# Ten products of zeros instead of six in TensorE's first step

## The chip, the cores and the metric

The kernel runs on one core of one Trainium2 chip. The metric is device time in microseconds (us) of one execution; the median of several runs is compared. A core has five engines that work side by side, each with its own queue of instructions in a fixed order: TensorE (PE in the profile) multiplies, VectorE (DVE) and ScalarE (ACT) work elementwise, GpSimd (POOL) and SyncE (SP) here mostly issue transfers (DMA). Engines wait for one another through semaphores.

## The reference

The computation mixes two branches over 2048 rows of 512 numbers, weighted row by row by a gate. Branch A is a filter in the frequency domain (a 2D real FFT, a product with complex weights, the inverse FFT). Branch B is two dense layers with a GELU between them.

```python
x = A_x                                              # 1 x 2048 x 512
g = sigmoid((x * gate_w).sum(-1, keepdims=True))
X = rfft2(x) * (A_w_r + 1j * A_w_i)                  # 2048 x 257
a = irfft2(X, s=(2048, 512))
h = gelu(x @ B_w1 + B_b1)                            # 512 -> 1792
b = h @ B_w2 + B_b2                                  # 1792 -> 512
out = g * a + (1 - g) * b
```

## The kernel before

The rows are tiled in 16 blocks of 128 (`NJ = 16`); four classes c = 0 to 3 hold the blocks j with j % 4 == c. The hidden width 1792 is cut in 14 slices f of 128. To keep float32 accuracy in a format that TensorE multiplies at one pass, each operand is split into a high and a low part (names ending in h and l): x into mxh and mxl, slice f of the first weight matrix into wa{f}h and wa{f}l. ScalarE or VectorE rounds the high part out of the loaded numbers, VectorE subtracts to get the low part, and a product is the sum of three: high by high, low by high, high by low. `ph` is the PSUM block in which the first dense layer of one slice accumulates. After it ScalarE applies the bias and the GELU (L904) and splits the result into g_{f}h (L466), and VectorE makes g_{f}l (L467). The FFT branch is done with matrix products too: folding adds on VectorE (`eo` and `w`, L571 and L574) and products into `pd` and `py`.

All work is recorded as steps. A table of numbers, ORDER, sets the order in which the steps are written out, and SLOTS says which buffer each tile gets. So every engine's queue is fixed by hand, and nothing is sorted at run time.

What matters here is the start. VectorE writes a tile of zeros (`zero`, L484), and TensorE's first step, `warm`, multiplies it by itself six times into a block `none` that nobody reads: 512 columns each. Ten more steps (`FILL`) hold one smaller product of zeros each, 256 columns; ORDER puts eight of them right after `warm` and two between the first groups for slice 0 and those for slice 1. Meanwhile the first transfers come in: four 128-row blocks of x that make up class 0 (blocks 0, 4, 8 and 12), the first weight slices (`war`, split into wa0h and so on, L890 to L896) and the first slices of the second matrix (`wb`). The weight for slice 0 comes in two halves, each turned into its half of wa0h by VectorE (L891). The first real products, eight of 128 columns, need both halves and blocks 0 and 4 of x; then come groups of four products with 256 columns (half of class 0), first for slices 0 and 1 with blocks 0 and 4, then the same with blocks 8 and 12, and from slice 2 on products of 512 columns.

All of TensorE's products outside branch B's last part are written by one helper, `mm` (L416), so that line stands beside most of TensorE's rows, and the tile names tell them apart.

Of the kernel before, what the change touches and what calls it, by code (L numbers as in the profile page):

```python
# [345 lines left out]
def tile_kernel(ctx: ExitStack, tc: tile.TileContext, xt, xc, w1, w2, b1, b2, x0g, wf, wrev, out, consts):  # L346
# [68 lines left out]
    def mm(ps, w, x, start, stop):  # L415
        pe.matmul(ps, w, x, start=start, stop=stop)  # L416
# [6 lines left out]
    def bcast(ap, *ns):  # L423
        return bass.AP(tensor=ap.tensor, offset=ap.offset, ap=[list(ap.ap[0]), *[[0, n] for n in ns], list(ap.ap[1])])
# [62 lines left out]
      -1).table = "gelu"  # L487

    def warm():
        for _ in range(6):  # L490
            mm(none.ap(), zero.ap(), bcast(zero.ap(), 4), True, True)

    add("pe", 2.65, 0.1, warm, [zero], [none], -2)

    for _ in range(FILL):
# [783 lines left out]
```

## Time and profile before

| | us |
|---|---|
| median of 3 runs | 366.76 |
| the three runs | 364.87, 366.76, 367.12 |
| span of the profiled execution, first to last instruction | 364.1 |
| TensorE's first product of zeros starts | 1.05 |
| its first real product starts | 7.04 |
| ScalarE's first GELU starts | 15.58 |

The profiled execution's own device time is not given with the profile; its span is what the profile tells of it. The profile gives the busy time of each engine, 40 slices of the span, the chain of work that ended last, and groups of instructions. A timeline lists the instructions of an engine by time: start and duration in us, engine, line, operation, output and inputs, the shapes, how many were merged into the row, and in brackets how long the engine sat idle before and what it waited for. A row that merges several products shows the shape of the first one. A product's duration includes its way through the array, so products that follow each other overlap in time, and the distance between starts tells the rate.

### The profile page before, as it was taken

The page shows a single profiled execution, that of the slowest core. Times are in us where ns is not written, and L with a number is a line of the kernel's source. Part 1 is how long each engine was busy: PE and PEld are TensorE (multiplying, and loading weights), DVE is VectorE, ACT ScalarE, POOL GpSimd, SP SyncE. Part 2 cuts the span into 40 slices and gives each one's busy share as a digit, 9 for nine tenths or more (in the row PEclk, how much of TensorE's full clock was granted, in tenths as well). Part 3 has the DMA queues.
Part 4 walks back from the last instruction along what each step waited for, and adds up shares of the span by engine and source line. Part 5 has one row for each costly group of instructions (what it writes and reads, how often), then busy time and mean ns, then how long its engine had stood idle before and what let it go on. Part 6 is the DMA issues. An engine that isn't in the chain of part 4 may idle for free.

```text
span 364.1 us, 5722 instructions
## 1 busy us (share of the span) xinstructions
PE 358.0 (98%) x1808; PEld 305.1 (84%) x1808; DVE 330.0 (91%) x745; ACT 254.1 (70%) x471; POOL 70.3 (19%) x91
## 2 busy tenths in 40 slices
PE   7999999999999999999999999999999999999996
PEld 6988898899878888888888888888888888889885
DVE  3588998998997899999999899999988889999995
ACT  4596579798988722257567865899999988676200
POOL 1011000121012132111023430010323221103220
PEclk9999999999999999999999999999999999999999
DMA  7997868568859699999978987164868858479878
GB/s 251 352 309 171 275 206 230 160 179 192 222 126 220 155 242 195 249 325 241 251 176 138 190 146 213 44 164 125 160 103 157 117 88 193 110 207 200 219 181 245
DMA packets 46494, 70.34 MB, mean 193 GB/s; under 512 B 5376, under 2 KB 19200, under 8 KB 46464
## 3 DMA queue, kind: packets, MB, share of 16 engines
q1 hardware_dynamic: 34592, 48.93, 42.2%
q0 software_dynamic: 11440, 20.72, 36.6%
q10 hardware_dynamic: 432, 0.33, 0.3%
q8 instruction: 14, 0.23, 0.2%
q14 instruction: 16, 0.13, 0.1%
HBM read 48.32 MB, written 19.41 MB: 186 GB/s over the span
## 4 chain that ended last, share of the span: by engine, by line
PE 97%; DMA 1%; SPq 0%; DVE 0%; issue 0%; DVEq 0%
PE ph L416 22%; PE poB L416 21%; PE po L416 21%; PE ux L1090 10%; PE nu L1090 8%; PE pd L416 4%; PE pz L416 4%; PE py L416 3%; PE pa L416 3%; DMA war<-in_w 1%; SPq L505 0%; PE pown L416 0%; PE none L416 0%; SPq L890 0%; DVE wa0h L891 0%
## 5 line engine op out<-in xcount | busy, mean ns | idle before, releaser
L904 ACT ACTIVATE ph<-ph,b1t 128x512 f32<-128x512 f32 x28 | 18.3, 654 | 17.1 <-PE ph L416 17.1
L407 POOL DMA_DIRECT2D bacc<-oB x16 | 14.2, 909 | 53.5 <-ACT oB L982 53.0
L803 ACT ACTIVATE sw<-y,al 64x512 f32<-64x512 f32 x32 | 22.9, 720 | 1.2 <-DVE y L669 0.7
L407 POOL DMA_DIRECT2D bacc<-o x16 | 14.9, 991 | 41.0 <-ACT o L982 38.2
L765 DVE TENSOR_TENSOR m<-y,wf 128x514 f32<-128x514 f32 x32 | 21.5, 691 | 0.2
L982 ACT ACTIVATE o<-po 128x512 f32<-128x512 f32 x16 | 9.3, 597 | 17.3 <-PE po L416 17.3
L632 ACT ACTIVATE y<-pys 64x257 f32<-64x257 f32 x32 | 13.4, 418 | 6.4 <-DVE pys L629 5.7
L416 PEld LDWEIGHTS pz<-tg,pq 128*128 128x128 f32 x128 | 16.8, 191 | 1.2
L416 PE MATMUL pd<-cf,w 128*128 128x129 f32 x128 | 17.8, 274 | 0.0
L416 PEld LDWEIGHTS pd<-cf,w 128*128 128x128 f32 x128 | 16.8, 190 | 0.8
L1090 PE MATMUL nu<-xf,wa0h 128*128 128x512 f32 x56 | 17.5, 394 | 0.0
L416 PE MATMUL py<-zb,tf 128*128 128x258 f32 x96 | 17.2, 294 | 0.0
L416 PE MATMUL pz<-tg,pq 128*128 128x128 f32 x128 | 17.2, 274 | 0.0
L810 DVE SCALAR_TENSOR_TENSOR pq<-y,al,sw 128x256 f32<-128x256 f32 x32 | 14.8, 478 | 0.9 <-ACT sw L803 0.7
L416 PEld LDWEIGHTS py<-zb,tf 128*128 128x128 f32 x96 | 14.3, 190 | 1.2
L416 PEld LDWEIGHTS pa<-zb,ci 128*128 128x128 f32 x96 | 13.9, 188 | 1.4
L416 PE MATMUL pa<-zb,ci 128*128 128x256 f32 x96 | 14.8, 283 | 0.0
L607 DVE TENSOR_TENSOR zb<-pd,zb 128x256 fp32r<-128x256 f32 x32 | 12.8, 419 | 0.8 <-ACT zb L604 0.7
L574 DVE TENSOR_TENSOR w<-eo 128x256 f32<-128x256 f32 x32 | 12.8, 419 | 0.3
L571 DVE TENSOR_TENSOR eo<-xf 128x256 f32<-128x256 f32 x32 | 12.9, 419 | 0.0
L823 DVE TENSOR_TENSOR zb<-pz,zb 128x512 fp32r<-128x512 f32 x16 | 10.9, 687 | 2.1 <-ACT zb L822 2.1
L604 ACT ACTIVATE zb<-pd 128x256 fp32r<-128x256 f32 x32 | 12.0, 382 | 1.1 <-PE pd L416 0.5
(700 smaller groups left out, 1277.6 us busy)
## 6 DMA issues: line engine op xcount, KB each, us to landing
wf<-in_wf SPq DMA_DIRECT2D x16, 257.0 KB
bacc<-o POOLq DMA_DIRECT2D x16, 256.0 KB, 6.1
bacc<-oB POOLq DMA_DIRECT2D x16, 256.0 KB, 5.4
xf<-in_xt SPq DMA_DIRECT2D x14, 256.0 KB
wr<-in_w SPq DMA_DIRECT2D x14, 256.0 KB, 4.4
tf<-tf SPq DMA_DIRECT2D x16, 192.0 KB, 4.5
bacc<-o SPq DMA_DIRECT2D x8, 256.0 KB, 5.5
ba<-bacc SPq DMA_DIRECT2D x8, 256.0 KB, 7.8
```

The costliest lines, as they stand in the source:

```text
L407: return add("pool", 2.3 * kb / 340, 3.4, lambda: nc.gpsimd.dma_start(dst(), src(), accum_op=ALU.add), reads, writes, rank)
L416: pe.matmul(ps, w, x, start=start, stop=stop)
L571: v(lambda s=s, op=op: vec.tensor_tensor(eo.ap()[:, s], x.ap()[:, 0:2], x.ap()[:, 2:4], op=op), 256, [x], [(eo, s)], feed)
L574: v(lambda s=s, op=op: vec.tensor_tensor(w.ap()[:, s], eo.ap()[:, :, 0], eo.ap()[:, :, 1], op=op), 256, [eo], [(w, s)], feed)
L604: a(lambda c=c: act.activation(segs(xh, c), both(c), AF.Copy), 256, [ps[c]], [(xh, c)], 0)
L607: v(lambda c=c: vec.tensor_tensor(segs(xl, c), both(c), segs(xh, c), op=ALU.subtract), 256, [ps[c], (xh, c)], [(xl, c)], 0)
L632: a(lambda o=o, i=i: act.activation(Y[j].ap()[o:o + HP, 1], pys.ap()[i:i + HP, 1], AF.Copy), 257, [(pys, 1)], [(Y[j], 1 + k)], 0, more=0.1)
L765: v(lambda mk=mk, k=k, y=y, w=w: vec.tensor_tensor(mk.ap(), y.ap(), w.ap()[:, k:k + 1, :ND].to_broadcast([P, 2, ND]), op=ALU.mult), 514, [ ...
L803: a(lambda sw=sw, y=y, o=o, i=i: act.activation(sw.ap()[o:o + HP], y.ap()[i:i + HP, ::-1, :HD], AF.Copy, scale=al.ap()[i:i + HP, 0:1]), 51 ...
L810: v(lambda sw=sw, pq_=pq_, y=y, j=j, k=k, op=op: vec.scalar_tensor_tensor(pq_.ap()[:, k], y.ap()[:, k, :HD], al.ap()[:, 1 + j:2 + j], sw.a ...
L904: a(lambda: act.activation(ps.ap(), ps.ap(), AF.Gelu_apprx_tanh, bias=b1t.ap()[:, f:f + 1]), 600, [b1t], [ps]).table = "gelu"
L1090: pe.matmul(o.ap(), w(wi, e), FX[j].ap()[:, xi, e], start=first, stop=k == 5, skip_group_check=not start)
```

## The change

One number is changed: `warm` issues ten products of 512 columns instead of six. All ten read `zero` and write `none`, as the six do. The step keeps its place, its two buffers and its planned cost.

```diff
     def warm():
-        for _ in range(6):
+        for _ in range(10):
             mm(none.ap(), zero.ap(), bcast(zero.ap(), 4), True, True)
 
     add("pe", 2.65, 0.1, warm, [zero], [none], -2)
```

TensorE's queue at the start of the program, before (a row is a run of equal products; x6 counts them, and the numbers at the end of a name are those of the buffers):

```order
L1271 UNCONDITIONAL_BRANCH
L416 MATMUL none<-zero 128x512 x6
L416 MATMUL none<-zero 128x256 x8
L416 MATMUL ph_0_137<-mxh_95,wa0h 128x128 x8
L416 MATMUL ph_0_137<-mxl_115,wa0h 128x256 x4
```

And now:

```order
L1271 UNCONDITIONAL_BRANCH
L416 MATMUL none<-zero 128x512 x10
L416 MATMUL none<-zero 128x256 x8
L416 MATMUL ph_0_141<-mxh_99,wa0h 128x128 x8
L416 MATMUL ph_0_141<-mxl_119,wa0h 128x256 x4
```

Only the count in the second row differs; the buffers' running numbers shift by four. Every later row of TensorE's queue, and every row of the other four queues, is the same but for such numbers.

## The prediction

> **What bounds the kernel now.** I read the page first: the busy table, the 40 slices, and the chain that ended last.
>
> ```profile
> PE 358.0 (98%) x1808; PEld 305.1 (84%) x1808; DVE 330.0 (91%) x745; ACT 254.1 (70%) x471; POOL 70.3 (19%) x91
> PE   7999999999999999999999999999999999999996
> PEclk9999999999999999999999999999999999999999
> PE 97%; DMA 1%; SPq 0%; DVE 0%; issue 0%; DVEq 0%
> ```
>
> TensorE is busy in every slice but the first and the last, and 97% of the chain is its work. The PEclk row reads full speed from the start; the durations below contradict it for the first 13 us, and I go by the durations. Next I read TensorE's timeline from the start of the span (columns: start, duration, instruction, count, idle time before it and what ended that).
>
> ```profile
> 1.05 4.64 PE L416 MATMUL none<-zero 128*128 128x512 f32 x14 [1.05 <-DVE zero L484]
> 7.04 1.94 PE L416 MATMUL ph<-mxh,wa0h 128*128 128x128 f32 x8 [1.35 <-DVE wa0h L891]
> 8.78 1.16 PE L416 MATMUL ph<-mxl,wa0h 128*128 128x256 f32 x4
> 9.73 1.05 PE L416 MATMUL ph<-mxh,wa0l 128*128 128x256 f32 x4
> 10.59 0.63 PE L416 MATMUL none<-zero 128*128 128x256 f32 x2
> 11.02 1.05 PE L416 MATMUL ph<-mxh,wa1h 128*128 128x256 f32 x4
> 11.87 1.05 PE L416 MATMUL ph<-mxl,wa1h 128*128 128x256 f32 x4
> 12.72 0.91 PE L416 MATMUL ph<-mxh,wa1l 128*128 128x256 f32 x4
> 13.47 0.64 PE L416 MATMUL ph<-mxh,wa0h 128*128 128x256 f32 x4
> 13.94 0.64 PE L416 MATMUL ph<-mxh,wa1h 128*128 128x256 f32 x4
> ...
> 16.34 0.40 PE L416 MATMUL ph<-mxh,wa2h 128*128 128x512 f32 x1
> 16.57 0.40 PE L416 MATMUL ph<-mxl,wa2h 128*128 128x512 f32 x1
> ```
>
> The starts tell the rate, since products overlap. Four products of 256 columns take 11.87 - 11.02 = 0.85 us, which is 0.213 us each; after 13.47 four take 0.47 us, 0.118 us each. The group that starts at 12.72 takes 0.75 us: three at the slow rate and one at the fast. So TensorE runs at about half rate until about 13.35 us, and no row before that is fast. The first stretch of unbroken work (1.05 to 5.69, 4.64 us) was not enough to end it; the second, from 7.04 on, was, after 13.35 - 7.04 = 6.31 us. Between them lie the 1.35 us in which TensorE waits for the second half of wa0h. That gap costs twice: its own length, which no edit here can win back because the weight is late, and, if unbroken work is what lifts the rate, a new start of that count.
>
> **The change part by part.** It adds four products of 512 columns to TensorE's queue between the sixth and the eight small ones, and nothing else; no wait, no DMA and no tile is added.
>
> *Their length.* At the slow rate 512 columns cost 2 x 0.213 = 0.425 us by spacing, so four cost 1.70 us. The other end is the whole duration of one such product, as if none overlapped:
>
> ```profile
> L416 PE MATMUL none<-zero x2: 628/628/628, 2.9 to 3.4; 128*128 128x512 f32 x2
> ```
>
> That gives 4 x 0.628 = 2.51 us, but two of them start 0.4 to 0.5 us apart in this same row, so I take 1.70. The stretch of zeros then ends at 5.69 + 1.70 = 7.39. Its last 0.20 us is drain (the two products at 10.59 last 0.63 us, and the next group starts 0.43 us after them), so the first real product can start at 7.19, against 7.04 before. Between 5.69 and 7.04 the four stand where nothing ran; 0.15 us of them lies on the path.
>
> *The rate.* TensorE now works without a gap from 1.05 us. The trace bounds how long that must last: 4.64 us was too short, 6.31 us was enough. So the full rate should come between 5.69 and 1.05 + 6.31 = 7.36 us, not at 13.35. If it comes early in that range, the small zero products shorten too, and the first real product starts at 7.04 as before. I take the late end, 7.36.
>
> [...]
>
> *What full rate is worth.* Now the inputs of the first real products decide, so their rows on VectorE and ScalarE:
>
> ```profile
> 6.60 0.29 DVE L891 CAST wa0h<-war 128x256 fp32r<-128x256 f32 x1 [2.17 <-DMA war<-in_w]
> 6.81 1.29 DVE L560 TENSOR_TENSOR mxl<-xf,mxh 128x512 fp32r<-128x512 f32 x2
> 8.35 0.69 DVE L896 TENSOR_TENSOR wa0l<-war,wa0h 128x512 fp32r<-128x512 f32 x1
> 9.28 0.69 DVE L896 TENSOR_TENSOR wa1l<-war,wa1h 128x512 fp32r<-128x512 f32 x1
> 9.88 1.29 DVE L560 TENSOR_TENSOR mxl<-xf,mxh 128x512 fp32r<-128x512 f32 x2
> ```
>
> None of these waits for TensorE, so they stay where they are. From the end of one to the product that needs it I allow 0.15 us (6.89 to 7.04 in the rows). Step by step: the eight products of 128 columns, 1.74 us before, take 0.87 and end at 8.06. The next four need mxl, ready at 8.10, and so start at 8.25 and end at 8.73. The next four need wa0l, ready at 9.04: they start at 9.19 and end at 9.66. The two zeros take 0.24, to 9.90. Three groups for wa1 take 0.47 each, to 11.31 (wa1l is ready at 9.97). That is the point that stands at 13.47 before: **2.16 us earlier**. The six groups after it are at full rate in both; the second pair of mxl is ready at 11.17 and is wanted about 12.3. So ph for wa2 starts at 14.18 instead of 16.34. Two waits for data (0.19 and 0.46 us) are inside this number, and they make it insensitive: a release anywhere up to about 7.5 us ends at the same 9.19.
>
> *Does it last to the end?* What is late next is whatever TensorE then reaches sooner. The rows where the other engines hand over:
>
> ```profile
> 15.58 0.66 ACT L904 ACTIVATE ph<-ph,b1t 128x512 f32<-128x512 f32 x1 [3.87 <-PE ph L416]
> 17.34 0.63 ACT L894 ACTIVATE wa3h<-war 128x512 fp32r<-128x512 f32 x1
> 16.90 0.69 DVE L467 TENSOR_TENSOR g_1l<-ph,g_1h 128x512 fp32r<-128x512 f32 x1 [3.20 <-ACT g_1h L466]
> 18.00 0.69 DVE L896 TENSOR_TENSOR wa3l<-war,wa3h 128x512 fp32r<-128x512 f32 x1 [0.41 <-ACT wa3h L894]
> 19.54 0.39 PE L416 MATMUL ph<-mxh,wa3l 128*128 128x512 f32 x1
> 6.17 0.33 SPq L893 DMA_DIRECT2D war<-in_w  x1
> 10.60 0.43 SPq L478 DMA_DIRECT2D xf<-in_xt  x1
> 22.94 0.62 ACT L559 ACTIVATE mxh<-xf 128x512 fp32r<-128x512 f32 x1
> tf<-tf SPq DMA_DIRECT2D x9, 192.0 KB, 5.3
> 7.00:20.00 13.00, 12.96 (x71) 12.35 (x72) 9.29 (x20) 8.80 (x15) 1.11 (x2) 1.00 1.06 366
> 120.00:364.00 244.00, 240.44 (x1178) 202.77 (x1176) 228.83 (x483) 159.92 (x280) 53.86 (x62) 1.00 0.79 179
> ```
>
> ScalarE had waited 3.87 us for TensorE's first finished block, and VectorE 3.20 us for ScalarE behind it. Both idle times exceed 2.16 us, so both queues move forward with TensorE. Among what moves is wa3h and wa3l, which stand behind those waits and are ready 0.85 us before TensorE wants wa3l (18.69 against 19.54); this margin stays if all three move together. Transfers are the part that does not move: from 7 to 20 us the DMA engines are full (share 1.06 in the stage row). The weight for wa3 is issued at 6.17 and used at 17.34, an x block is issued at 10.60 and used by ScalarE at 22.94, so 11 to 12 us lie between; loads of this kind land in about 5.3 us. With 2.16 us taken away the cover holds. Later the DMA share falls to 0.79 and TensorE is busy 240.44 of 244 us, so there is room to keep the lead. The loss on the way is bounded by 0 and 2.16 us; as both idle times and both transfer margins are larger than the shift, I take 0.
>
> **Sum.** The profiled execution spans 364.1 us, 2.66 less than the median of 366.76; its own device time is not given, and I take 2.66 as what lies around the span. 364.1 - 2.16 + 2.66 = **364.6 us**, 0.6% below the median. A difference of 1% is about what a measurement of this kernel can tell from none, so this counts as no change.
>
> **The rivals.**
>
> *A. The forecast:* release before 7.5 us, lead kept. 364.6 us, with its own range 364.0 to 365.4.
>
> *B. The lead is lost on the way.* TensorE arrives early at a block whose weights or x data have not come. For it speak the full DMA engines from 7 to 20 us and VectorE's 91%; against it the margins above. If ScalarE did not follow, the margin of 0.85 us at wa3l would be all that is kept: 366.76 - 0.85 = 365.9 us. If nothing is kept, 366.8.
>
> *C. The change does not do what it says:* products of zeros do not count as work, or the release depends on something else, so the half rate ends 6.31 us after the first real product as before. Then 0.15 us of delay remains, 366.9 us. For it speaks that 4.64 us of zeros released nothing; against it, that they were shorter than the stretch that did.
>
> *D. Slower than before:* the added zeros hold the queue. If they cost their full 0.628 us each, the stretch ends at 8.20, the first real product starts at 8.00, 0.96 us late, and with no earlier release the time is 367.7 us. In general a delay of 0.15 us is repaid as soon as the release comes before 13.05 us, twice 0.15 ahead of 13.35.
>
> *E. The median is not like this trace.* The three times before are 364.87, 366.76 and 367.12; the spread of 2.25 us is about the size of my sum. If the half rate ends early in some executions already, the changed kernel is always like the fastest: 364.9 us, and it is steadier rather than much faster. [...] It lies in A's range.
>
> **How the numbers follow.** Chances: A 0.44, E 0.30, B 0.12, C 0.08, D 0.03, and 0.03 for a lead that grows or a chip that differs by more. To leave out no more than 2 in 10, the range takes A and E and most of B: 363.8 to 366.4 us. None of the cases reaches 1% (363.1 or 370.4 us): faster 0.03, within 1% 0.95, slower 0.02.
>
> **What would show it.** The zeros' row should have 18 products and last from 1.05 to about 7.2; groups of four 256-column products should start 0.47 us apart from the first one on; TensorE should wait for mxl near 8.1 and for wa0l near 9.0; the first product with wa2h should start near 14.2, ScalarE's first L904 near 13.4, and the span should be near 361.9. The forecast is wrong in its mechanism if spacings of 0.85 us still stand after 8 us, and wrong in its last step if wa2h starts near 14.2 but the span is over 363.

## The result, and the profile after

| | us |
|---|---|
| predicted | 364.6 (363.8 to 366.4) |
| measured, median of 7 runs | 363.98 (363.27 to 364.53) |
| kernel before, median of the 7 runs in all | 365.88 (364.55 to 367.12) |
| ratio after to before | 0.9948, 95% interval 0.9926 to 0.997 |
| span of the profiled execution after | 362.6, in a run of 364.53 |

The change saves half a per cent, and the interval excludes no change. The profiled execution is the slowest of the seven. The busy table of the page and its chain of work, after:

```profile
PE 356.9 (98%) x1812; PEld 303.1 (84%) x1812; DVE 330.1 (91%) x745; ACT 254.2 (70%) x471; POOL 70.3 (19%) x91
PE 91%; DMA 4%; SPq 1%; ACT 1%; DVE 1%; issue 1%; DVEq 0%; ACTq 0%
```

TensorE has four products more (1812 against 1808) and is busy 1.1 us less (356.9 against 358.0): work that ran slowly now runs faster. The chain names some DMA and ScalarE now, which comes up again below. TensorE's timeline at the start, after:

```profile
1.05 5.61 PE L416 MATMUL none<-zero 128*128 128x512 f32 x18 [1.05 <-DVE zero L484]
7.34 1.08 PE L416 MATMUL ph<-mxh,wa0h 128*128 128x128 f32 x8 [0.68 <-DVE wa0h L891]
8.45 0.74 PE L416 MATMUL ph<-mxl,wa0h 128*128 128x256 f32 x4
9.39 0.74 PE L416 MATMUL ph<-mxh,wa0l 128*128 128x256 f32 x4 [0.20 <-DVE wa0l L896]
9.97 0.40 PE L416 MATMUL none<-zero 128*128 128x256 f32 x2
10.21 0.64 PE L416 MATMUL ph<-mxh,wa1h 128*128 128x256 f32 x4
10.69 0.64 PE L416 MATMUL ph<-mxl,wa1h 128*128 128x256 f32 x4
14.53 0.40 PE L416 MATMUL ph<-mxh,wa2h 128*128 128x512 f32 x1
```

The groups of four products start 0.48 us apart from 10.21 on; before, they were 0.85 us apart until 12.72. The first row holds the moment of the change: at the slow rate 18 products would last 4.64 + 1.70 = 6.34 us, and they last 5.61. The 0.73 us saved, at 45% saved per unit of slow work (0.118 against 0.213 us), is 1.6 us of slow work done fast, so the rate rose near 7.2 - 1.6 = 5.6 us. That is 4.6 us after TensorE's start, about as long as the whole stretch that had not been enough before. And there still is a gap of 0.68 us before the first real product. So it is not that the added products leave TensorE no idle time before the real work; the experiments ask what they do instead.

### The profile page after: what moved, and what is told of

It is laid out like the page before. It is cut to its first block, busy times and chain, and to the rows that moved or that the text cites. A ratio compares the mean times of both kernels' runs of the same rounds, so it can differ in the third digit from the quotient of the medians.

```text
span 362.6 us, 5730 instructions
## 1 busy us (share of the span) xinstructions
PE 356.9 (98%) x1812; PEld 303.1 (84%) x1812; DVE 330.1 (91%) x745; ACT 254.2 (70%) x471; POOL 70.3 (19%) x91
## 4 chain that ended last, share of the span: by engine, by line
PE 91%; DMA 4%; SPq 1%; ACT 1%; DVE 1%; issue 1%; DVEq 0%; ACTq 0%
PE poB L416 21%; PE po L416 20%; PE ph L416 17%; PE ux L1090 11%; PE nu L1090 8%; PE pd L416 4%; PE pz L416 4%; PE py L416 3%; PE pa L416 3%; DMA bacc<-o 3%; DMA war<-in_w 1%; ACT gb L1199 0%; SPq L877 0%; SPq L657 0%; DVE mxl L560 0%
```

## The experiments

Four theories, all of them conjectures of the author's when they were put down. Theory 1: the rate is decided at the ends of windows of about 3.41 us (the distance between the two changes of the clock in w10nofill, 9.27 and 12.68) that run on regardless of the program; a busy window raises it, a window with much idle time lowers it. Theory 2: unbroken work is counted, and a gap starts the count again (the prediction's reading of the trace). Theory 3: the rate has no part in it, and the zeros merely keep TensorE at hand. Theory 4: a certain number of zeros is needed. In all diffs below the kernel after is the base, unless it says otherwise. The runs come in two series on two chips (w0, w24, late6 and w10nofill on one; b6, w8, w10 and w14 on the other), each with the kernel before beside them, so times are compared within a series. The ratios are those on record; they are not exactly the quotients of the medians.

### No large product, and far too many

```diff
-        for _ in range(10):
+        for _ in range(0):     # w0
+        for _ in range(24):    # w24
```

> No 512-column products of zeros; the eight small ones stay, so the first stretch of work is only about 2 us (1.05 to 3). Theory 1 (the full rate begins at the end of the first free-running window of some 3.4 us that TensorE worked through): the first stretch can never hold a window, so the rate rises 3.4 to 6.8 us after the first real product at about 7.2, that is between 10.6 and 14, in every execution; time 365.3 to 367, median about 366.3, slower than before in the mean by up to 0.6 us and slower than the changed kernel by about 2.3. Theory 2 (unbroken work is counted, 4.6 us at least and 6.3 at most, and a gap starts the count again): the rate rises at 11.8 to 13.5, time as before, 365.9. Theory 3 (the time is won by the zeros being there when data come, not by the rate): all 256-column groups after 8 us still 0.47 us apart here, time as changed, 364.

> 24 products of 512 columns. By every theory of the rate it is full before 7.9 us, while the zeros run to about 9.6 us instead of 6.7, so the first real product comes about 2.3 us late. The groups behind it no longer wait for mxl and wa0l, which gives back 0.8 us. Expected 1.4 us behind the changed kernel: 365.4. If a late start were hidden by later waits for data, it would be 364.0.

Measured: w0 366.16 us (12 runs), against 365.19 for the kernel before in the same series (35 runs, 362.68 to 367.98), ratio 1.0022, interval 0.9999 to 1.0046. w24 365.44 us, ratio 1.0014, interval 0.9992 to 1.0036. TensorE's rows, first of w0, then of w24:

```profile
1.05 2.08 PE L416 MATMUL none<-zero 128*128 128x256 f32 x8 [1.05 <-DVE zero L484]
6.54 1.94 PE L416 MATMUL ph<-mxh,wa0h 128*128 128x128 f32 x8 [3.40 <-DVE wa0h L891]
11.37 1.05 PE L416 MATMUL ph<-mxl,wa1h 128*128 128x256 f32 x4
12.22 0.97 PE L416 MATMUL ph<-mxh,wa1l 128*128 128x256 f32 x4
13.03 0.64 PE L416 MATMUL ph<-mxh,wa0h 128*128 128x256 f32 x4
13.51 0.64 PE L416 MATMUL ph<-mxh,wa1h 128*128 128x256 f32 x4
```

```profile
1.05 8.38 PE L416 MATMUL none<-zero 128*128 128x512 f32 x32 [1.05 <-DVE zero L484]
9.28 1.01 PE L416 MATMUL ph<-mxh,wa0h 128*128 128x128 f32 x8
10.12 0.69 PE L416 MATMUL ph<-mxl,wa0h 128*128 128x256 f32 x4
10.65 0.64 PE L416 MATMUL ph<-mxh,wa0l 128*128 128x256 f32 x4
15.69 0.40 PE L416 MATMUL ph<-mxh,wa2h 128*128 128x512 f32 x1
```

In w0 the first real product starts early, at 6.54, and yet its groups stay 0.85 us apart until about 13: theory 3 falls. In w24 there is no gap and no wait for data left, every real product runs at full rate, and the first product for wa2h starts 1.16 us later than in the profiled kernel after, though its weight landed 0.56 us earlier (6.34 against 6.90 for the second half of wa0h); the time is what was expected. So the zeros beyond the landing of the weight cost 1.94 us at the first real product (9.28 against 7.34) and 1.16 us at wa2h (15.69 against 14.53): the way between the two, without waits for data, is 0.78 us shorter. The times of these two runs do not separate theories 1 and 2, but the trace of w24 speaks against theory 2: its rate rose at 4.68 us (by the clock records further down), after 3.6 us of unbroken work, where theory 2 needs more than the 4.64 us that had not been enough before.

### The same six products, without their gap

This one starts from the kernel before: `zero` is written nine times, so TensorE begins later, with the same 14 products of zeros.

```diff
-    add("vec", 0.3, 0.1, lambda: vec.memset(zero.ap().bitcast(F32), 0.0), [], [zero], 0)
+    add("vec", 0.3, 0.1, lambda: [vec.memset(zero.ap().bitcast(F32), 0.0) for _ in range(9)], [], [zero], 0)
```

> Six products as before, but the tile of zeros is written nine times, so TensorE starts about 1.4 us later (near 2.4) and works without a gap until the first real product: the same work as before, without its gap. Theory 1: the window that counts may straddle the first real products; the full rate comes between 5.8 and 9.2 us, mostly before the wait for wa0l at 9.3 ends; time 364.0 to 364.5, as the changed kernel. Theory 2: 2.4 + 4.6 to 6.3, so 7.0 to 8.7; 364.0 to 364.3. Theory 4 (the amount of zeros decides, ten are needed): the rate rises as before, time 365.9.

Measured: 364.09 us (12 runs, 363.76 to 365.41), 1.1 us below the 365.19 of the kernel before; ratio 0.9988, interval 0.9968 to 1.0008, which alone does not settle it. The profile shows more:

```profile
3.12 4.63 PE L416 MATMUL none<-zero 128*128 128x512 f32 x14 [3.12 <-DVE zero L484]
7.56 1.04 PE L416 MATMUL ph<-mxh,wa0h 128*128 128x128 f32 x8
8.43 0.69 PE L416 MATMUL ph<-mxl,wa0h 128*128 128x256 f32 x4
14.17 0.40 PE L416 MATMUL ph<-mxh,wa2h 128*128 128x512 f32 x1
```

The zeros start at 3.12 (the writes took longer than the 1.4 us assumed) and run at the slow rate throughout (4.63 us, against 4.64 in the kernel before), but the real products behind them are fast from the first, and wa2h stands at 14.17 instead of 16.34. By the clock records further down the rate rose at 7.62, as the real products began. No product was added. Theory 4 falls: six are enough here, where no gap follows them.

### Ten products, with the gap

```diff
-    for _ in range(FILL):
-        add("pe", 0.22, 0.0, lambda: mm(none.ap()[:, :2], zero.ap(), bcast(zero.ap(), 2), True, True), [zero], [none], 0)
+    for k in range(FILL):
+        add("pe", 0.22, 0.0, lambda k=k: k < 8 or mm(none.ap()[:, :2], zero.ap(), bcast(zero.ap(), 2), True, True), [zero], [none], 0)
```

> Ten products of 512 columns, but the eight small ones after them left out: the first stretch lasts from 1.05 to about 5.5, no longer than the 4.64 us before, with the gap of about 1.5 us before the first real product. Theory 1: a stretch of 4.25 to 4.5 us holds a whole window in about 3 of 10 executions; the times scatter between 364 and 367, median 366. Theory 2: as before, 365.9, the rate rises 4.6 to 6.3 us after the first real product. Theory 4 (ten products are enough): 364.

Measured: 365.17 us (12 runs, 362.72 to 366.79), ratio to the kernel before 0.9998, interval 0.9969 to 1.0026: ten large products alone show no gain. Theory 1 had put the median at 366; it came out lower. TensorE's rows, and then its busy time by stages (columns: stage and length, busy us and number of products, granted clock, DMA share, GB/s):

```profile
1.05 4.63 PE L416 MATMUL none<-zero 128*128 128x512 f32 x10 [1.05 <-DVE zero L484]
7.10 1.08 PE L416 MATMUL ph<-mxh,wa0h 128*128 128x128 f32 x8 [1.41 <-DVE wa0h L891]
8.21 0.74 PE L416 MATMUL ph<-mxl,wa0h 128*128 128x256 f32 x4
9.15 1.14 PE L416 MATMUL ph<-mxh,wa0l 128*128 128x256 f32 x4 [0.20 <-DVE wa0l L896]
11.37 1.05 PE L416 MATMUL ph<-mxl,wa1h 128*128 128x256 f32 x4
15.77 0.40 PE L416 MATMUL ph<-mxh,wa2h 128*128 128x512 f32 x1
```

```profile
9.20:10.00 0.80, 0.80 (x4) 0.54 1.06 405
10.00:12.60 2.60, 2.60 (x14) 0.50 1.03 374
12.60:16.00 3.40, 3.40 (x29) 0.99 1.04 336
```

Here the rate is full at 7.10, after the gap, and falls back to a half while TensorE is working. The clock column can be read here, because the profile records a change: 0.54 in the stage of 0.80 us means full for 8% of it, so it fell at 9.26; 0.99 in the last stage means half for 2% of 3.40 us, so it rose at 12.67. That is 3.41 us later. Theory 2 falls: the only interruption near is the wait of 0.20 us before the product at 9.15, and the kernel after has the same wait before its product at 9.39 and keeps its rate. Theory 1 names the window that ended there, from 5.86 on, which held most of the gap.

### The kernel before, profiled again

> The kernel before, unchanged, for a second profile. Theory 1: its release falls at another time than 13.35 us, anywhere from 4.5 to 5.7 us or 10.4 to 13.9 us, and may be taken back once; time 362.7 to 368, as the 35 executions on the last chip. Theory 2 (a count of unbroken work): the rate rises 6.3 us after the first real product again, near 13.4.

Measured: 365.6 us (8 runs, 364.8 to 366.62). The same program as in the first profile, and another history:

```profile
1.05 3.91 PE L416 MATMUL none<-zero 128*128 128x512 f32 x14 [1.05 <-DVE zero L484]
7.23 1.83 PE L416 MATMUL ph<-mxh,wa0h 128*128 128x128 f32 x8 [2.27 <-DVE wa0h L891]
11.10 1.05 PE L416 MATMUL ph<-mxh,wa1h 128*128 128x256 f32 x4
16.77 0.40 PE L416 MATMUL ph<-mxh,wa2h 128*128 128x512 f32 x1
```

```profile
7.23:8.86 1.63, 1.63 (x8) 0.54 1.06 395
8.86:13.66 4.80, 4.80 (x23) 0.50 1.06 396
13.66:16.00 2.34, 2.34 (x19) 0.89 1.03 325
```

The 14 zeros last 3.91 us instead of 4.64, so the rate rose near 3.9 us. With the weight 0.19 us later, that lengthened the gap from 1.35 to 2.27 us, and the clock fell again at 7.23 + 0.08 x 1.63 = 7.36, to come back at 13.66 + 0.22 x 2.34 = 14.17, 6.81 us later: twice 3.41. So the early rise does not help this execution of the kernel before: the rate fell behind the gap of 2.27 us.

In two points this is not what theory 1 had forecast. The rate rose before 4.5 us, at the end of a window that began 0.53 us ahead of TensorE's first product. And it came back a window late: from 7.35 to 10.76 us TensorE has no idle time in its rows, and yet that window did not raise the rate. So the busy time of the rows alone does not tell which window raises the rate; more on this below, under what stays open.

### Eight, ten and fourteen

```diff
-        for _ in range(10):    # w10: the kernel after, unchanged
+        for _ in range(8):     # w8
+        for _ in range(14):    # w14
```

> The changed kernel again, beside the others of this series on one chip. Theory 1 (free windows of 3.41 us; the rate rises when one was busy enough and falls back when one held too much idle time): its first stretch lasts about 5.6 us and its gap 0.7 us; the rate rises between 4.5 and 7.9 us; median about 364.0, nearly all executions between 363.3 and 364.6. If the gap of 0.7 us is sometimes enough to take the rate away, single executions reach 365 to 366.

> Eight products of 512 columns: first stretch 1.05 to about 6.2, gap 0.6 to 1.0 us. Theory 1: a whole window fits into the first stretch in about half the executions, and of the rest some have a window that straddles a gap short enough; times scatter between 363.5 and 366.5, median about 364.5, between six and ten. A theory in which ten products are a threshold: as six, 365.2 to 365.9.

> 14 products of 512 columns, so that the zeros reach past the landing of the weight at 7.0 to 7.4 and no gap is left. Theory 1: the rate rises between 4.5 and 7.9 us and cannot fall again; the first real product starts at 7.3 to 7.9, and the wait for wa0l hides that; 364.0, with the same floor as ten products but no stragglers. If every extra product beyond the gap costs its length (0.23 us at full rate), 364.5.

| products | median us | runs | from | to | ratio to before, interval |
|---|---|---|---|---|---|
| 6 (before) | 365.71 | 21 | 364.45 | 366.68 | |
| 8 | 364.35 | 10 | 363.22 | 364.57 | 0.9959 (0.9944 to 0.9974) |
| 10 | 363.49 | 6 | 363.07 | 363.92 | 0.9947 (0.9929 to 0.9964) |
| 14 | 363.93 | 6 | 363.28 | 364.12 | 0.9956 (0.994 to 0.9972) |

TensorE's first rows with eight and with fourteen:

```profile
1.05 5.49 PE L416 MATMUL none<-zero 128*128 128x512 f32 x16 [1.05 <-DVE zero L484]
7.30 1.08 PE L416 MATMUL ph<-mxh,wa0h 128*128 128x128 f32 x8 [0.75 <-DVE wa0h L891]
```

```profile
1.06 6.15 PE L416 MATMUL none<-zero 128*128 128x512 f32 x22 [1.06 <-DVE zero L484]
7.04 1.01 PE L416 MATMUL ph<-mxh,wa0h 128*128 128x128 f32 x8
8.69 0.74 PE L416 MATMUL ph<-mxh,wa0l 128*128 128x256 f32 x4
```

Every execution with ten lies below every execution of the kernel before in this series. Eight came out better than expected: the times do not scatter to 366.5. Its zeros run at the slow rate to the end (5.49 us is 4.64 + 0.85), yet the real products are fast from 7.30, though 0.75 us without work precede them: by the clock records the rate rose at 6.98, in the middle of that pause. So a window with 0.44 us of idle time in it (from 3.57 to 6.98, the zeros ending at 6.54) still raised the rate. Fourteen close the gap and show no gain over ten; the intervals do not tell the three apart. The gap left with ten, 0.48 us in this series' profile and 0.68 us in the first, did not bring the half rate back.

### The clock of every execution

A result gives each execution's mean granted clock. One lost window, 3.41 us at half rate in 364, lowers it by 0.5 x 3.41 / 364 = 0.0047, to 0.995; half rate before the first rise does not show (the first profile before has 1.000, with half rate up to 13.31), and at the very end of the span up to 0.002 is missing in some (w10 and w14 have 0.998, and their records fall at 359.80 and 359.78, 1.7 and 1.6 us before the end). So a clock of 0.995 or less marks an execution in which the rate rose early and was taken back (the profiled executions of w10nofill and b6 have 0.995 and 0.991).

| kernel, series | executions | taken back (clock 0.991 to 0.995) |
|---|---|---|
| before, second series | 35 | 19 |
| before, third series | 21 | 9 |
| ten without the small ones | 12 | 4 |
| before, profiled again (b6), third series | 8 | 5 |
| none (w0) | 12 | 0 |
| twenty-four (w24) | 12 | 0 |
| six, started late (late6) | 12 | 0 |
| eight, ten, fourteen | 22 | 0 |
| after, first series | 7 | 0 |

The first series is that of the result, the second that of w0, the third that of w10. In w0, whose profile shows no early rise, nothing was taken back, and its median is the highest of its series; in the kernels that come out fast the profiles show an early rise that stays. In the second series the fastest six of the kernel before (362.68 to 363.54) have 0.998 or 0.999, so nothing was taken back there; that the rate had risen early is inferred from their times, for executions of w0 have such clocks too.

Each trace also keeps the granted clock as a list of stretches, each with its start, its length and its share of full speed (us from the span's start):

| run | the clock changes at | full rate then lasts |
|---|---|---|
| before, first profile | up 13.31 | 351.57 |
| after | up 5.62 | 358.40 |
| w0 | up 12.96 | 351.57 |
| w24 | up 4.68 | 358.40 |
| late6 | up 7.62 | 354.99 |
| w10nofill | up 5.86, down 9.27, up 12.68 | 351.57 |
| b6 | up 3.94, down 7.35, up 14.18 | 351.57 |
| w8 | up 6.98 | 354.99 |
| w10 | up 4.81 | 354.99 |
| w14 | up 4.79 | 354.99 |

The long stretches, each up to the fall behind the last work (364.88 in the first profile before, whose last product ends at 360.44; 364.02 after, where it ends at 359.00), are 103, 104 or 105 times 3.413 us, which is also the length of the single stretches in w10nofill. So the windows of theory 1 show in these records: they run on through the whole execution, and they lie elsewhere in each, with changes for instance at 13.31 in the first profile of the kernel before and at 3.94, 7.35 and 14.18 in its second.

## Why the prediction was right

**The mechanism, half rate at the start that the added products end earlier, was right**, and the value of ending it nearly so. What makes the rate rise was reasoned wrongly, and that the time came so close is partly luck. The steps one by one:

*Length of the added products.* Taken as 1.70 us; the row of zeros grew by 0.97 us (5.61 against 4.64). The rate rose only when nearly all of the ten large ones were through (5.62 us), but the eight small ones behind them ran fast. The first real product was not delayed by them: it waits for wa0h (0.68 us of idle time in its row), whose half landed later in this execution.

*When the rate rises.* The forecast was 5.69 to 7.36 us, by a count of unbroken work; it rose at 5.62. The time does not hang on this, since by the prediction's own working a release anywhere up to about 7.5 us gives the same sum; but the reason given was wrong. Work of 4.64 us is not too short: the second profile of the same kernel rose 2.9 us after TensorE's start, before its stretch of zeros was over. What the records show instead are changes 3.41 us apart in w10nofill, 3.41 and 6.83 us apart in b6, and at another place in each execution. And after a rise a gap can cost the rate again: behind gaps of 1.41 us (ten without the small ones) and 2.27 us (kernel before) the half rate came back, behind 0.68 us (after) it did not.

*What full rate is worth.* Forecast 2.16 us earlier at wa2h; measured 16.34 - 14.53 = 1.81. The rows on VectorE explain the rest:

```profile
6.90 0.29 DVE L891 CAST wa0h<-war 128x256 fp32r<-128x256 f32 x1 [2.40 <-DMA war<-in_w]
8.65 0.68 DVE L896 TENSOR_TENSOR wa0l<-war,wa0h 128x512 fp32r<-128x512 f32 x1
13.77 0.66 ACT L904 ACTIVATE ph<-ph,b1t 128x512 f32<-128x512 f32 x1 [1.73 <-PE ph L416]
```

The weight's second half came 0.30 us later than in the profile before (6.90 against 6.60), and wa0l with it. The prediction let this row stay where it was; over the ten profiled executions it starts anywhere from 6.10 to 6.90. Taken from there, the forecast of 14.18 becomes 14.48, against 14.53. ScalarE's first GELU followed, 1.81 us earlier, and its wait for TensorE shrank from 3.87 to 1.73 us: that idle time was longer than the shift, as the prediction said.

*Does the lead last?* Taken as 0 lost. By the span behind the first wa2h product it was 364.1 - 16.34 = 347.8 us before and 362.6 - 14.53 = 348.1 after, 0.3 lost. The loss has a place:

```profile
119.91 0.60 ACT L466 ACTIVATE g_7h<-ph 128x512 fp32r<-128x512 f32 x1 [2.24 <-DMA bacc<-o]
123.76 0.50 PE L416 MATMUL po<-g_5h,wb5h 128*128 128x512 f32 x1 [0.18 <-ACT o L982]
DMA to landing us min/median/max: 4.1/6.2/10.8
```

A write to bacc takes 10.8 us to land here (9.4 before). Before, g_7h started at 121.33, so it came forward by 1.42 instead of 1.81 us, and through ScalarE's queue TensorE waits 0.18 us for a block to be emptied; that product starts 0.57 us after the one ahead of it (123.19), where 0.23 is usual. So rival B happened, at a fifth of the lead, and not by a load near the start, where the prediction had looked, but by a write at 109 us. It is not bound to the number of products: in the other profiled executions the same difference is 347.6 in w10 (ten as well), w0, w14, w24 and b6, 347.9 in w8, 348.1 in late6 and 348.7 in w10nofill.

*The sum.* The term that was mis-sized is the time around the span, 2.66 us, taken from a median of three runs. After, a run of 364.53 has a span of 362.6, so 1.9 us. With that the forecast's own terms give 364.1 - 2.16 + 1.9 = 363.8, against 363.98; and the profiled execution before comes to 366.0, next to the median of seven, 365.88. That 364.6 stands against 364.53 in the profiled execution after is luck: its span was forecast near 361.9 and is 362.6 (0.35 us by the later wa2h, the rest by the lead lost), and these 0.7 us too little cancel the 0.76 us too much around the span.

*The rivals.* C and D did not occur: the rate rose during the zeros (5.62 us, with the first real product at 7.34), and no delay arose; w24 shows what D would cost with 24 products: 1.35 us over late6 in the same series. E was right that the executions before differ among themselves (364.45 to 366.68 in one series, 362.68 to 367.98 in another), but in the third series, with 21 executions before and 6 with ten, none of the 21 was as fast as the slowest with ten.

What stays open is how much of a window must be worked through to raise the rate or to keep it. With windows laid in steps of 3.41 us from the clock's changes, their idle times by TensorE's rows are these. At half rate, windows with 0.17 (w10nofill), 0.44 (w8) and 0.53 us (b6, its first) raised the rate; windows with none (b6, from 7.35), 0.40 (w0) and 0.56 us (the first profile before) did not, nor did any with 0.79 us or more. So idle time in the rows alone does not decide. The three named that failed all hold the first real products, eight of 128 columns, which take about 0.21 us each at half rate (1.74 us for eight in the first profile before, 1.63 in b6), as long as products of 256 columns (0.85 us for four). Whether that kept the rate down is not shown: no run tests it. At full rate, a window with 0.7 us without work kept it (after), and windows with 1.44 (w10nofill, 1.24 of it before the first real product) and 2.27 us (b6) lost it. These are placements by arithmetic, one execution each, and no run varied the idle time alone.

## What to carry to other kernels

Filling TensorE's first microseconds was here not a matter of reaching a number of products (six were enough in late6), but of leaving no window of 3.41 us with a long pause (1.44 us was too long, 0.7 us was not), from the first product until real work flows. The lengths are those of this kernel's runs. End the filler a little before the first operands land rather than well after: here ten products left 0.5 to 0.7 us of idle time and were no slower than fourteen, which left none, while 24 products took 1.35 us more than six that began late. And read the rate from the distance of starts; one profile shows one position of the windows (the rate first rose at 13.31 us in one execution of the kernel before and at 3.94 in another), so take a second before building on when the rate changes.

## What the runs showed of the hardware

That the half rate can come back while TensorE is working was not expected: the clock fell at 9.27 (ten without the small ones) and at 7.35 us (the kernel before, profiled again), with TensorE back at work, for a pause that was already over. In the second case the next 3.41 us of work without a pause did not bring it back; 6.83 us did. Nor was it that raising the rate early can be in vain: fast zeros end sooner (3.91 against 4.64 us), so in the second profile of the kernel before the gap grew from 1.35 to 2.27 us (0.73 of it by the faster zeros) and was long enough to lose the rate again. The page's clock row reads 1.00 where products are plainly at half rate (0.85 us for four, in the stage from 9.20 to 13.30 us of the first profile before), up to the first change on record; after one, it agreed with the distances (0.50 where four products take 0.85 us, in w10nofill from 10.00 to 12.60).
